# Output weights of the last batch loaded into free quarters of the input weights, with the order of all engines redone

## The chip, the core and the metric

The kernel runs on one core of a Trainium2 chip. The metric is the device time in microseconds (us). Five engines work side by side, each through its own list of instructions: TensorE (PE, with its weight loads listed apart as PEld), VectorE (DVE), ScalarE (ACT), GpSimd (POOL) and SyncE (SP). SP does nothing but issue the transfers between DRAM and the on-chip memory, one after the other; an instruction that waits holds up everything behind it on its engine.

## The reference, cut to what matters

Four batches of 8 heads, 768 positions, head width 64. Attention looks at a window of 16 positions and at one summary for each block of 32 (the largest key, the mean value). Its output x (768 x 512 in each batch) goes through a gated layer:

```python
h = np.maximum(x @ w_in, 0.0)                 # 512 -> 1024
u, v = h[..., :512], h[..., 512:]
v_n = (v - mu) / np.sqrt(var + 1e-06)         # over the 512
v_s = w_spatial @ v_n + b_spatial[:, None]    # mixes the 768 positions
return (u * v_s) @ w_out                      # 512 -> 512
```

## The kernel before, in words

Every operand of a large product is split into a high and a low part, and each product is made of three matmuls: high by high, high by low, low by high. `mm3` (L698 to L714) issues them, so all large products are at line 712: pv and pu are the halves v and u of x @ w_in, q the product with w_spatial, po the product with the output weights. Attention has lines of its own: s the scores (L401), p their softmax (L417 to L432), t a transposition of p (L443), x the product with the values (L462).

PE works on a batch's gated layer while the next batch's attention runs on the other engines. The gated layers of batches 1 to 3 make the product with w_spatial (`spatial_s`) from seven smaller products, whose combinations of w_spatial ("pieces" 0 to 6) were stored in DRAM as scr0 to scr6 and are loaded again in each batch, 1,152 KB each, into `arena`, a ring of three slots (`piece_load`). The load of a piece can be issued when the piece three before it has been used for the last time. The output weights wo were stored as scr7 and scr8 and are loaded again too. In the last batch before the change, the first half of them (d = 0 and 1) is an eighth piece of the ring; the other half (d = 2 and 3) goes into two tiles `wt` that take the place of a part of x.

The last batch also uses another form of the product x @ w_in, in which combinations of quarters of w_in are loaded from scw tensors into quarters of `win_h` and `win_l` (the high and low parts of w_in), and into `swv`. `gate` (L919 to L925) multiplies u into c and splits the result into gt for po.

What every engine does, and in which order, comes from one list of numbers, `ORDER`, over all operations (2,111 before), with `OTHER`, the set of operations that go to their second-choice engine. Buffers are given out in the same order. SP's transfers stand in this list as well; each waits, in turn, for its buffer and for the transfer issued eight before it.

Of the kernel before, what the change touches and what calls it, by code (L numbers as in the profile page):

```python
# [9 lines left out]
F32 = mybir.dt.float32  # L10
# [139 lines left out]
def tile_local_summary_attention_gmlp(ctx: ExitStack, tc: tile.TileContext, qT, kext, vpad, vnat, vT, w_in, w_sp, b_rep, w_out, out):  # L150
# [552 lines left out]
    def mm3(ps, n, steps, pri, *hold, first=True, skip=False):  # L703
# [185 lines left out]
    def spatial_s(b, pri, step):  # L889
# [65 lines left out]
        for n, i in enumerate((0, 1, 2, 3, 4, 5, 6, 7) if last else (0, 1, 2, 5, 6, 3, 4, 7, 8)):  # L955
# [38 lines left out]
        half = lambda x, d: (x, lambda w, cs: x.t[:, (d * 2 + w) * DM:(d * 2 + w + 1) * DM][:, cs])  # L994
        s["wo"] = [half(ar[7 + d // 2], d % 2) for d in range(2 if last else NC)]
        for d in range(2, NC if last else 2):
            x = Buf(att, [P, 2, 2 * CH], F32R, "x01l", f"wt{b}_{d}")
            mark("wt", b, d)
            dma(lambda x=x: x.t.rearrange("p w n -> p (w n)").bitcast(F32), scr[8][:, (d - 2) * 2 * DM:(d - 1) * 2 * DM], 512, pri + AR_AT,
                w=[x], r=[("scr", 8, w, 0) for w in range(2)] + [(u, f, c) for f in range(NC) for c in range(2)])  # L1000
            s["wo"].append((x, lambda w, cs, x=x: x.t[:, w, cs]))

    def proj_out(b, t, pri):
# [4 lines left out]
                             [gh[th, d][0], gl[th, d][0], gh[th, d][2], gl[th, d][2], s["wo"][d][0]]) for d in range(NC)] if b else [((lambda d=d: gh[th, d][1]()[:, o:o + P], lambda d=d: gl[th, d][1]()[:, o:o + P], lambda d=d: wo_h[:, d, cs], lambda d=d: wo_l[:, d, cs]),  # L1008
# [327 lines left out]
```

## Time and profile before

| | |
|---|---|
| median of 3 runs (lowest, highest) | 390.93 us (390.2, 393.24) |
| time of the profiled execution | 390.44 us |
| span in its trace | 388.6 us |
| PE busy | 377.7 us, 97% |
| PEld busy | 333.5 us, 86% |
| DVE busy | 280.6 us, 72% |
| ACT busy | 236.2 us, 61% |
| POOL busy | 154.2 us, 40% |
| granted TensorE clock | 1.00 in each stretch read below |

The span runs from the first to the last instruction; 1.8 us of the time lie around it. A busy share is an average over the whole span. In a timeline, each row gives the start, the length, the engine, the line and operation, the tiles, and in square brackets the idle time of the engine before it with what ended that. Matmuls overlap, so the length of one is more than what it adds: that is read from the distance between the starts.

### The profile page before, as it was taken

To read this page: it belongs to the slowest core of one execution; us is meant where nothing else is said; L and a number is where in the kernel's file an instruction comes from. 1 tells how busy PE (TensorE), PEld (TensorE's weight loads), DVE (VectorE), ACT (ScalarE), POOL (GpSimd) and SP (SyncE) were. 2 spreads that over 40 slices of the span, in tenths; PEclk is the share of its full clock that TensorE was granted. 3 is DMA by queue.
4 is the path that set the end of the run, shared out by engine and by line. 5 is a ranking of instruction groups with operands and counts; after the bars stand their busy time and mean duration, and the time that the engine had idled before them with its cause. 6 is when DMAs were issued, how large, how long until landed. Compare 5 with 4: busy or idle time off the path is not lost.

```text
span 388.6 us, 9377 instructions
## 1 busy us (share of the span) xinstructions
PE 377.7 (97%) x3382; PEld 333.5 (86%) x3382; DVE 280.6 (72%) x881; ACT 236.2 (61%) x716; POOL 154.2 (40%) x196
## 2 busy tenths in 40 slices
PE   8889999999999999999999999999999999999896
PEld 8658888888898888889998888899998799999885
DVE  4989898798876169787884658686787669785710
ACT  2999999876764756587463584756438555370212
POOL 4151455323573053424466143454644332623400
PEclk9999999999999999999999999999999999999999
DMA  8999997997788869979899737878899172949403
GB/s 286 406 281 279 287 347 212 293 258 237 266 230 251 279 216 340 314 231 331 312 306 335 179 102 253 296 216 326 284 291 316 76 253 91 339 167 357 188 30 133
DMA packets 38591, 99.05 MB, mean 255 GB/s; under 512 B 3601, under 2 KB 17937, under 8 KB 35217
## 3 DMA queue, kind: packets, MB, share of 16 engines
q1 hardware_dynamic: 38544, 98.45, 77.8%
q8 instruction: 27, 0.44, 0.5%
q14 instruction: 20, 0.16, 0.1%
HBM read 77.59 MB, written 20.84 MB: 253 GB/s over the span
## 4 chain that ended last, share of the span: by engine, by line
PE 79%; DMA 8%; DVE 5%; ACT 5%; issue 1%; SPq 1%; DVEq 0%; ACTq 0%
PE pv L712 16%; PE pu L712 16%; PE po L712 15%; PE q L712 13%; PE x L462 6%; PE s L401 5%; PE sp L712 4%; PE t L443 4%; DMA arena<-scr 4%; DMA vt<-in_vT_dram 3%; ACT p L421 3%; DMA k<-in_kext_dram 2%; DVE p L417 1%; DVE p L432 1%; SPq L216 1%
## 5 line engine op out<-in xcount | busy, mean ns | idle before, releaser
L421 ACT ACTIVATE p<-p,sums 128x120 f32<-128x120 f32 x192 | 73.9, 389 | 8.4 <-DVE sums L417 7.9
L432 POOL TENSOR_TENSOR p<-p,sums 128x480 f32<-128x480 f32 x34 | 34.8, 1040 | 52.0 <-DVE sums L428 44.8
L417 DVE CUSTOM_DVE_ANT_0 p<-s,mask 128x120 f32<-128x120 f32 x192 | 42.6, 276 | 10.0 <-PE s L401 10.0
L712 PE MATMUL po<-arena,gt 128*128 128x512 f32 (+1 forms) x168 | 40.3, 385 | 1.5 <-DMA arena<-scr 1.5
L712 PE MATMUL q<-arena,vnh 128*128 128x384 f32 x144 | 37.1, 338 | 0.0
L712 PEld LDWEIGHTS po<-arena,gt 128*128 128x128 f32 x168 | 30.3, 188 | 7.7 <-issue 1.8
L421 ACT ACTIVATION_READ_ACCUMULATOR p<-p,sums 128x1 f32 x192 | 36.8, 192 | 0.0
L712 PE MATMUL pu<-xh,win_h 128*128 128x512 f32 (+1 forms) x96 | 33.1, 345 | 0.0
L712 PE MATMUL pu<-xl,win_h 128*128 128x512 f32 (+1 forms) x96 | 32.4, 337 | 0.0
L712 PE MATMUL pu<-xh,win_l 128*128 128x512 f32 (+1 forms) x96 | 32.3, 337 | 0.0
L712 PE MATMUL q<-arena,wo_hl 128*128 128x384 f32 x144 | 29.9, 339 | 0.2 <-DMA arena<-scr 0.2
L712 PE MATMUL pv<-win_h,xh 128*128 128x512 f32 x72 | 29.9, 415 | 0.0
L712 PE MATMUL pv<-win_h,xl 128*128 128x512 f32 x72 | 28.2, 392 | 0.0
L712 PE MATMUL pv<-win_l,xh 128*128 128x512 f32 x72 | 28.2, 392 | 0.0
L443 PE MATMUL t<-ident,p 128*120 128x128 f32 x192 | 27.3, 274 | 0.9 <-POOL p L432 0.4
L462 PEld LDWEIGHTS x<-pt,ve 120*64 120x64 f32 x768 | 23.6, 138 | 5.2 <-issue 1.2
L222 ACT COPY pt<-t 120x512 f32<-120x512 f32 x36 | 20.8, 586 | 12.1 <-PE t L443 11.7
L921 POOL TENSOR_TENSOR c<-c,u 128x384 f32<-128x384 f32 x17 | 17.7, 1046 | 26.2 <-DVE c L938 17.0
L443 PEld LDWEIGHTS t<-ident,p 128*120 128x120 f32 x192 | 22.0, 137 | 5.6 <-POOL p L432 1.4
L462 PE MATMUL x<-pt,ve 120*64 120x64 f32 x768 | 25.5, 224 | 1.1 <-ACT ob_t3h L526 0.7
L712 PEld LDWEIGHTS q<-arena,vnh 128*128 128x128 f32 x144 | 25.6, 188 | 0.3 <-DVE sums L417 0.2
L712 PEld LDWEIGHTS q<-arena,wo_hl 128*128 128x128 f32 x144 | 24.9, 188 | 1.1 <-DVE ob_y L949 0.5
(274 smaller groups left out, 987.8 us busy)
## 6 DMA issues: line engine op xcount, KB each, us to landing
arena<-scr SPq DMA_DIRECT2D x21, 1152.0 KB, 6.3
k<-in_kext_dram SPq DMA_DIRECT2D x16, 544.0 KB, 7.7
qd<-in_qT_dram SPq DMA_DIRECT2D x24, 256.0 KB, 6.4
ve<-in_vpad_dram SPq DMA_DIRECT2D x24, 256.0 KB, 7.1
out_dram<-ob SPq DMA_DIRECT2D x23, 256.0 KB, 2.1
arena<-scr SPq DMA_DIRECT2D x5, 1024.0 KB, 7.6
vt<-in_vT_dram SPq DMA_DIRECT2D x12, 384.0 KB, 4.8
scr<-ct SPq DMA_DIRECT2D x12, 384.0 KB, 3.7
```

Source lines behind the costliest of these rows:

```text
L216: add(("SP", issue), lambda e: nc.sync.dma_start(out=out_() if callable(out_) else out_, in_=in_() if callable(in_) else in_), pri, w, r, ...
L222: (nc.scalar.copy if e == "ACT" else nc.vector.tensor_copy)(out=out_, in_=in_)
L401: nc.tensor.matmul(out=ps[a].t[r * QB:(r + 1) * QB, i * KW:(i + 1) * KW], lhsT=qt[hs, r, i], rhs=kts[r].t[hs, g * SEG:g * SEG + KW], start ...
L417: add(("DVE", 205), lambda e, i=i, mi=mi, a=a, pt=pt, k=k: nc.vector.tensor_tensor_reduce(out=at(pt, i), in0=ps[a].t[:, i * KW:(i + 1) * K ...
L421: add(("ACT", 380), lambda e, i=i, pt=pt, k=k: nc.scalar.activation(out=at(pt, i), in_=at(pt, i), func=AF.Exp, scale=-1.0, bias=st.t[:, 0, ...
L432: add(dict(DVE=590, POOL=950), lambda e, a=a, pt=pt: eng(e).tensor_tensor(out=four(pt), in0=four(pt), in1=st.t[:, 0, a * BPU:(a + 1) * BPU ...
L443: nc.tensor.transpose(out=ps.t[:KW, i * P:(i + 1) * P], in_=pt.t[:, i * KW:(i + 1) * KW], identity=ident)
L462: nc.tensor.matmul(out=x.t[a * D:(a + 1) * D, r * CH + n * QB:r * CH + (n + 1) * QB], lhsT=ve[buf][:, n, o:o + D], rhs=tt[a].t[:KW, n * P ...
L712: nc.tensor.matmul(out=ps.t[:, :n], lhsT=x, rhs=y, start=(first and j == i == 0), stop=(j == last and i == 2), skip_group_check=skip)
L921: add(two_ns(HT), lambda e: eng(e).tensor_mul(out=g.t[:, :HT], in0=g.t[:, :HT], in1=u.t[:, d, ts]), pri, w=[g], r=[u, (u, d, 0), (u, d, th ...
```

## The change

In the last batch, the output weights are no longer loaded into the ring and into `wt`. They come in eight transfers of 256 KB, high and low part of each d, into quarters of `win_h` and `win_l` whose last use is over; the ring has seven pieces. `mm3` gives its output a matching shape where the right operand has three dimensions (128 x 2 x 256), as these quarters have. In the last batch, `gate` waits for both halves of u. `ORDER` (now 2,116 operations) and `OTHER` are replaced as a whole, for all four batches.

```diff
@@ weight
-            return at, [*keys, *[f"wi{half}_{k}_0{w}" for k in range(int(n[2]) - 1, NC, 2) for w in "hl"]]
+            return at, [("home", half, n), *keys, *[f"wi{half}_{k}_0{w}" for k in range(int(n[2]) - 1, NC, 2) for w in "hl"]]
@@ mm3
+                o = ps.t[:, :n]
+                if len(rh.shape) == 3 > len(lh.shape):
+                    o = o.rearrange("p (k n) -> p k n", k=rh.shape[1])
-                    nc.tensor.matmul(out=ps.t[:, :n], lhsT=x, rhs=y, start=(first and j == i == 0), stop=(j == last and i == 2), skip_group_check=skip)
+                    nc.tensor.matmul(out=o, lhsT=x, rhs=y, start=(first and j == i == 0), stop=(j == last and i == 2), skip_group_check=skip)
@@ gate
-            add(..., r=[u, (u, d, 0), (u, d, th)], port=True)
+            add(..., r=[u, (u, d, 0), (u, d, 1 if last else th)], port=True)
@@ spatial_s
-        for n, i in enumerate((0, 1, 2, 3, 4, 5, 6, 7) if last else (0, 1, 2, 5, 6, 3, 4, 7, 8)):
+        for n, i in enumerate((0, 1, 2, 3, 4, 5, 6) if last else (0, 1, 2, 5, 6, 3, 4, 7, 8)):
...
-        s["wo"] = [half(ar[7 + d // 2], d % 2) for d in range(2 if last else NC)]
-        for d in range(2, NC if last else 2):
-            x = Buf(att, [P, 2, 2 * CH], F32R, "x01l", f"wt{b}_{d}")
-            dma(lambda x=x: x.t.rearrange("p w n -> p (w n)").bitcast(F32), scr[8][:, (d - 2) * 2 * DM:(d - 1) * 2 * DM], 512, pri + AR_AT,
-                w=[x], r=[("scr", 8, w, 0) for w in range(2)] + [(u, f, c) for f in range(NC) for c in range(2)])
+        if not last:
+            s["wo"] = [half(ar[7 + d // 2], d % 2) for d in range(NC)]
+            return
+        for d, (h, i, r, gone) in enumerate(((1, 1, 0, ("sw", 1, 4)), (0, 0, 0, ("home", 0, "a11")), (0, 0, 1, ("home", 0, "a12")), (0, 1, 0, ("sw", 0, 2)))):
+            base = h * DF + i * HD
+            for w, x in enumerate((win_h, win_l)):
+                at = (d % 2 * 2 + w) * DM
+                dma(x[:, r::2, base:base + HD].bitcast(F32), scr[7 + d // 2][:, at:at + DM].rearrange("p (k n) -> p k n", k=2), 256, pri + AR_AT,
+                    w=[("wt", d, w), gone], r=[("scr", 7 + d // 2, w, 0), *[("scw", h, n) for n in range(1, 5)]])
+            def of(w, cs, r=r, base=base):
+                x = (win_h, win_l)[w][:, r::2, base:base + HD]
+                return x if cs.stop - cs.start == DM else x[:, cs.start // HD]
@@ tables
 ORDER = [
-    0, 1, 2, 3, 6, 8, 7, 84, 9, 47, 10, 85, 48, 49, 108, 143, 101, 52, 11, 19, 25, 23, 13, 21, 17, 15, 54, 53, 12, 26, 24, 86, 18, 14, 87, 88, 89, 55,
+    1, 2, 6, 8, 7, 84, 9, 47, 3, 0, 10, 85, 48, 49, 108, 143, 101, 52, 53, 23, 24, 86, 21, 25, 13, 19, 14, 11, 17, 12, 22, 18, 26, 87, 15, 16, 54, 88,
...
```

Three places show what the new order does. The first is SP's queue in the last batch, from its last input-weight quarter to its last weight load (arena<-scr1 to scr6 are pieces, scr7 and scr8 the output weights). Before:

```order
L216 DMA win_l_124<-scw04_141 128x2x256
L216 DMA arena_125<-scr1_130 128x2304
L216 DMA arena_125<-scr2_131 128x2304
L216 DMA arena_125<-scr3_132 128x2304
L216 DMA wt3_3_4697<-scr8_137 128x1024
L216 DMA wt3_2_4717<-scr8_137 128x1024
L216 DMA arena_125<-scr4_133 128x2304
L216 DMA arena_125<-scr5_134 128x2304
L216 DMA arena_125<-scr6_135 128x2304
L216 DMA arena_125<-scr7_136 128x2048
```

After the change, the twelve rows that end with the last load of weights:

```order
L216 DMA arena_125<-scr2_131 128x2304
L216 DMA win_h_123<-scr8_137 128x2x256
L216 DMA win_l_124<-scw04_141 128x2x256
L216 DMA win_h_123<-scr7_136 128x2x256
L216 DMA win_l_124<-scr7_136 128x2x256 x2
L216 DMA arena_125<-scr3_132 128x2304
L216 DMA win_l_124<-scr8_137 128x2x256
L216 DMA win_h_123<-scr8_137 128x2x256
L216 DMA arena_125<-scr4_133 128x2304
L216 DMA arena_125<-scr5_134 128x2304
L216 DMA arena_125<-scr6_135 128x2304
L216 DMA win_l_124<-scr8_137 128x2x256
```

The two loads into `wt` and the eighth piece, which stood last, are gone. Eight loads of quarters stand between the pieces; the first of them, win_h_123<-scr7_136, is two rows ahead of this piece of the list. Nothing but the last low quarter stands behind piece 6 (scr6).

The second is PE at the end of batch 3's attention, up to its last product x3_2 (po2 are output tiles of batch 2; p3_2 and t3_2 the last softmax and its transposition, which pt3_2 carries to x3_2). Before:

```order
L712 MATMUL po2_5_4057<-arena_125,gt2_1_1_3822 128x512 x3
L712 MATMUL po2_5_4057<-arena_125,gt2_1_2_3959 128x512 x3
L443 MATMUL t3_2_1_1_4067<-ident_78,p3_2_1_1_3965 120x128 x4
L712 MATMUL po2_4_4040<-arena_125,gt2_1_2_3959 128x512 x3
L712 MATMUL po2_3_4047<-arena_125,ob_gt2_1_3_3982 128x512 x3
L443 MATMUL t3_2_0_0_4094<-ident_78,p3_2_0_0_3976 120x128 x4
L443 MATMUL t3_2_1_0_4099<-ident_78,p3_2_1_0_3967 120x128 x4
L443 MATMUL t3_2_0_1_4108<-ident_78,p3_2_0_1_3969 120x128 x4
L712 MATMUL po2_4_4040<-arena_125,ob_gt2_1_3_3982 128x512 x3
L712 MATMUL po2_5_4057<-arena_125,ob_gt2_1_3_3982 128x512 x3
L712 MATMUL po2_2_4139<-arena_125,gt2_0_0_4084 128x512 x3
L462 MATMUL x3_2_0_4152<-pt3_2_0_0_4150,ve0_148 64x64
```

After:

```order
L715 MATMUL po2_4_4037<-arena_125,gt2_1_2_3981 128x512 x3
L715 MATMUL po2_3_4054<-arena_125,gt2_1_1_3834 128x512 x3
L715 MATMUL po2_3_4054<-arena_125,gt2_1_2_3981 128x512 x3
L715 MATMUL po2_3_4054<-arena_125,ob_gt2_1_3_3958 128x512 x3
L443 MATMUL t3_2_1_0_4070<-ident_78,p3_2_1_0_3968 120x128 x4
L443 MATMUL t3_2_0_0_4092<-ident_78,p3_2_0_0_3966 120x128 x4
L715 MATMUL po2_5_4041<-arena_125,ob_gt2_1_3_3958 128x512 x3
L443 MATMUL t3_2_0_1_4105<-ident_78,p3_2_0_1_3971 120x128 x4
L443 MATMUL t3_2_1_1_4110<-ident_78,p3_2_1_1_3973 120x128 x4
L715 MATMUL po2_4_4037<-arena_125,ob_gt2_1_3_3958 128x512 x3
L715 MATMUL po2_0_4139<-arena_125,gt2_0_0_4080 128x512 x3
L462 MATMUL x3_2_0_4143<-pt3_2_0_0_4100,ve0_148 64x64
```

The first group of t stood behind 24 matmuls of po2, and now all four stand behind 30 of them, within one group of po2 of one another. Behind the last t there are 6 matmuls of po2, where there were 9. On DVE, three operations of gt2 and one of ob_t1 stood between p3_2_0_1 and the copy pt3_2_0_0; now that copy follows p3_2_0_1 directly, and the copy pt3_2_0_1, before on ACT, comes on DVE behind one operation of gt2.

The third is SP near the start (vt holds the values from which the block means come, ve the values for the product x, qd the queries, wi and vn parts of w_in and of the values). Before:

```order
L216 DMA wi0_2_280<-in_w_in_dram 128x1024
L216 DMA vn_277<-in_vnat_dram 128x1536
L216 DMA ve0_148<-in_vpad_dram 32x4x256
L216 DMA vt1_0_428<-in_vT_dram 128x768
L216 DMA ve0_148<-in_vpad_dram 64x4x256
L216 DMA qd0_146<-in_qT_dram 128x512
L216 DMA ve1_149<-in_vpad_dram 64x4x256
L216 DMA ve1_149<-in_vpad_dram 32x4x256
L216 DMA qd1_147<-in_qT_dram 128x512
```

After:

```order
L216 DMA wi0_2_283<-in_w_in_dram 128x1024
L216 DMA vn_280<-in_vnat_dram 128x1536
L216 DMA qd1_147<-in_qT_dram 128x512
L216 DMA vt1_0_439<-in_vT_dram 128x768
L216 DMA ve0_148<-in_vpad_dram 64x4x256
L216 DMA ve0_148<-in_vpad_dram 32x4x256
L216 DMA qd0_146<-in_qT_dram 128x512
L216 DMA ve1_149<-in_vpad_dram 64x4x256
L216 DMA ve1_149<-in_vpad_dram 32x4x256
```

The third load of qd1 stood last of the nine, and now stands ahead of vt1_0, all four of ve and qd0. It waits for the scores s0_1_1, which read the buffer that it fills.

In the last batch on PE, twelve matmuls of pu3_7_0 and pu3_5_0 (6 each, 128x384), which stood ahead of the q3_2, now stand among the q3_3, between the last use of the slot that piece 4 takes and the first use of piece 4.

## Rows read from the trace of the kernel before

**Rows 1.** Windows by stage: length, then busy us (x instructions) of each engine, PEclk, DMA share, GB/s.

```profile
0.00:40.00 40.00, 35.54 (x474) 28.55 (x474) 32.42 (x144) 31.55 (x107) 14.02 (x35) 1.00 0.98 316
40.00:290.00 250.00, 249.86 (x2325) 219.77 (x2323) 188.28 (x576) 161.63 (x488) 110.52 (x123) 1.00 0.84 269
290.00:310.00 20.00, 19.00 (x149) 15.90 (x148) 14.68 (x62) 13.29 (x54) 6.81 (x7) 1.00 0.66 202
...
350.00:370.00 20.00, 18.30 (x102) 17.41 (x102) 13.19 (x25) 4.01 (x8) 8.26 (x8) 1.00 0.69 260
```

**Rows 2.** Waits of PE, whole span: us in total, times, longest.

```profile
PE po L712 <- DMA arena<-scr: 1.5, 1, 1.5
PE s L401 <- DVE sums L428: 0.9, 1, 0.9
...
PE q L712 <- DMA arena<-scr: 0.2, 1, 0.2
```

**Rows 3.** Timeline of PE, end of the last batch.

```profile
356.58 0.34 PE L712 MATMUL q<-arena,vnl 128*128 128x384 f32 x1
357.13 3.36 PE L712 MATMUL q<-arena,wo_hl 128*128 128x384 f32 x18 [0.22 <-DMA arena<-scr]
...
366.09 0.51 PE L712 MATMUL q<-arena,vnh 128*128 128x384 f32 x2
366.44 0.34 PE L712 MATMUL q<-arena,vnl 128*128 128x384 f32 x1
368.26 3.68 PE L712 MATMUL po<-arena,gt 128*128 128x512 f32 x15 [1.48 <-DMA arena<-scr]
371.78 0.84 PE L712 MATMUL po<-wt,gt 128*128 128x512 f32 x3
372.46 0.84 PE L712 MATMUL po<-arena,gt 128*128 128x512 f32 x3
...
384.15 0.52 PE L712 MATMUL po<-wt,gt 128*128 128x256 f32 x3
384.51 0.52 PE L712 MATMUL po<-wt,ob_gt 128*128 128x256 f32 x3
```

**Rows 4.** Chain that ended last, its transfers at the end.

```profile
350.70 6.29 DMA arena<-scr
...
360.52 7.60 DMA arena<-scr
```

**Rows 5.** DMA issues by kind: count, KB each, median us to landing.

```profile
win_h<-scw SPq DMA_DIRECT2D x5, 256.0 KB, 3.4
win_l<-scw SPq DMA_DIRECT2D x5, 256.0 KB, 5.6
```

**Rows 6.** Timeline of PE at the end of batch 3's attention.

```profile
303.41 0.84 PE L712 MATMUL po<-arena,gt 128*128 128x512 f32 x3
304.95 2.09 PE L462 MATMUL x<-pt,ve 120*64 120x64 f32 x64 [0.70 <-ACT ob_t3h L526]
```

**Rows 7.** Timeline of DVE at the same place.

```profile
301.35 2.57 DVE L931 TENSOR_TENSOR gt<-c,gt 128x384 fp32r<-128x384 f32 x3
303.84 0.41 DVE L528 TENSOR_TENSOR ob_t<-xt,ob_t 128x256 fp32r<-128x256 f32 x1
304.17 0.68 DVE L222 COPY pt<-t 120x512 f32<-120x512 f32 x1
```

**Rows 8.** Timeline of SP near the start.

```profile
15.83 1.19 SPq L216 DMA_DIRECT2D vt<-in_vT_dram  x1
...
21.63 0.33 SPq L216 DMA_DIRECT2D qd<-in_qT_dram  x1
```

**Rows 9.** Timeline of PE near the start.

```profile
20.36 1.17 PE L401 MATMUL s<-k,qd 64*64 64x120 f32 x32 [0.93 <-DVE sums L428]
...
28.08 1.15 PE L462 MATMUL x<-pt,ve 120*64 120x64 f32 x32 [0.35 <-DVE sums L417]
```

**Rows 10.** Timeline of DVE near the start.

```profile
26.71 0.95 DVE L367 TENSOR_REDUCE vs_in<-vt 128x24 f32<-128x768 f32 x1 [0.58 <-DMA vt<-in_vT_dram]
```

More of the change, by code (lines that the diff above doesn't have):

```diff
@@ L920, in gate @@
             ts = slice(th * HT, (th + 1) * HT)
-            add(two_ns(HT), lambda e: eng(e).tensor_mul(out=g.t[:, :HT], in0=g.t[:, :HT], in1=u.t[:, d, ts]), pri, w=[g], r=[u, (u, d, 0), (u, d, th)], port=True)
+            add(two_ns(HT), lambda e: eng(e).tensor_mul(out=g.t[:, :HT], in0=g.t[:, :HT], in1=u.t[:, d, ts]), pri, w=[g], r=[u, (u, d, 0), (u, d, 1 if last else th)], port=True)
             if b == B - 1 and (th, d) in ((1, 0), (1, 1)):
@@ L993, in spatial_s @@
                 leave(m, 0, 1, 0)
-        half = lambda x, d: (x, lambda w, cs: x.t[:, (d * 2 + w) * DM:(d * 2 + w + 1) * DM][:, cs])
-        s["wo"] = [half(ar[7 + d // 2], d % 2) for d in range(2 if last else NC)]
-        for d in range(2, NC if last else 2):
-            x = Buf(att, [P, 2, 2 * CH], F32R, "x01l", f"wt{b}_{d}")
-            mark("wt", b, d)
-            dma(lambda x=x: x.t.rearrange("p w n -> p (w n)").bitcast(F32), scr[8][:, (d - 2) * 2 * DM:(d - 1) * 2 * DM], 512, pri + AR_AT,
-                w=[x], r=[("scr", 8, w, 0) for w in range(2)] + [(u, f, c) for f in range(NC) for c in range(2)])
-            s["wo"].append((x, lambda w, cs, x=x: x.t[:, w, cs]))
+        half = lambda x, d: ([x], lambda w, cs: x.t[:, (d * 2 + w) * DM:(d * 2 + w + 1) * DM][:, cs])
+        if not last:
+            s["wo"] = [half(ar[7 + d // 2], d % 2) for d in range(NC)]
+            return
+        s["wo"] = []
+        for d, (h, i, r, gone) in enumerate(((1, 1, 0, ("sw", 1, 4)), (0, 0, 0, ("home", 0, "a11")), (0, 0, 1, ("home", 0, "a12")), (0, 1, 0, ("sw", 0, 2)))):
+            base = h * DF + i * HD
+            for w, x in enumerate((win_h, win_l)):
+                mark("wt", d, w)
+                at = (d % 2 * 2 + w) * DM
[4 more added lines that the diff above has]
+                return x if cs.stop - cs.start == DM else x[:, cs.start // HD]
+            s["wo"].append(([("wt", d, 0), ("wt", d, 1)], of))
     def proj_out(b, t, pri):
@@ L1007, in proj_out @@
         steps = lambda cs: [((lambda d=d: gh[th, d][1]()[:, o:o + P], lambda d=d: gl[th, d][1]()[:, o:o + P], lambda d=d: s["wo"][d][1](0, cs), lambda d=d: s["wo"][d][1](1, cs)),
-                             [gh[th, d][0], gl[th, d][0], gh[th, d][2], gl[th, d][2], s["wo"][d][0]]) for d in range(NC)] if b else [((lambda d=d: gh[th, d][1]()[:, o:o + P], lambda d=d: gl[th, d][1]()[:, o:o + P], lambda d=d: wo_h[:, d, cs], lambda d=d: wo_l[:, d, cs]),
+                             [gh[th, d][0], gl[th, d][0], gh[th, d][2], gl[th, d][2], *s["wo"][d][0]]) for d in range(NC)] if b else [((lambda d=d: gh[th, d][1]()[:, o:o + P], lambda d=d: gl[th, d][1]()[:, o:o + P], lambda d=d: wo_h[:, d, cs], lambda d=d: wo_l[:, d, cs]),
                              [gh[th, d][0], gl[th, d][0], gh[th, d][2], gl[th, d][2], f"wo{d}h", f"wo{d}l"]) for d in range(NC)]
```

171 rows, old and new, of tables (ORDER, OTHER) are left out of this document.

## The prediction, as it was put down before the result

> **What bounds the kernel now.** The windows by stage come first [rows 1]. PE is busy for 249.86 of the 250 us from 40 to 290, at a granted clock of 1.00, so between these marks nothing but fewer or shorter matmuls could make the time shorter, and the change takes out none. What PE loses lies in three places: 4.46 us of the first 40 (where the DMA share is 0.98: the inputs are arriving), 1.00 us from 290 to 310, and 1.70 us from 350 to 370. The list of PE's waits [rows 2] then names the causes: the longest single one is po waiting 1.5 us for a transfer into the ring; others are between 0.2 and 0.9 us. So the room is small: 4.46 + 0.14 + 1.00 + 1.70 = 7.3 us at the very most, 1.9% of the time, and the first of these includes the start, where PE has no data yet. Last come the timelines of the places where a wait lies, since a share of busy time says nothing of them.
>
> **The end of the last batch: -2.0 us.** The step from one matmul to the next is read from starts: two 128x384 matmuls take 366.44 - 366.09 = 0.35 us, so 0.175 each; three 128x512 take 372.46 - 371.78 = 0.68, so 0.227 each; three 128x256 take 384.51 - 384.15 = 0.36, so 0.12 each [rows 3]. The last q starts at 366.44 and the first po at 368.26: 1.82, of which 0.175 is its own step, so 1.65 us are lost. The chain says why: the eighth piece, which holds half of the output weights, is issued at 360.52, when its slot comes free, and takes 7.60 us [rows 4]. That piece is gone. Its part comes in quarters, which are issued ahead of pieces 3 to 6, or just behind. The only one behind piece 6, a low quarter, can be issued when the q3_3 that frees piece 6's slot are done. From there to the first po there are 18 q with piece 4 and most of 36 more, some 50 x 0.175 = 8.8 us, and a quarter of this shape landed in 3.4 (high) or 5.6 us (low) [rows 5]. Some 3 us are left over, so the wait is not replaced.
>
> The other loss is 357.13 - 356.58 = 0.55, less a step of 0.175, so 0.38 us, for piece 4: its load takes 6.29 us [rows 4], and the 36 q between the release of its slot and its first use cover 36 x 0.175 = 6.3. Twelve pu of 128x384 now stand among these: 12 x 0.175 = 2.1 us of cover. That ends this wait and leaves about 2 us for the eight quarters, which share the engines. In all 1.65 + 0.38 = 2.0 us go. The bounds are 0 (another transfer is late instead) and 2.1.
>
> The bytes are the same 2 MB (1,024 KB and two of 512 KB before, eight of 256 KB now). What the pieces lose to them is bounded by the 2 us of cover. The DMA share is 0.69 from 350 to 370 and the last piece's 1,024 KB are no longer in it [rows 1, 4], so I count nothing. The Trainium skill, DMA: Bandwidth & Descriptors, section Measured, speaks against this part: it advises batches of at least 1 MiB for 75% of the peak, with 64 KB at 32%. Between those two, an estimate of 55% for 256 KB would make the 2 MB take some 2.6 us longer (8.7 against 6.1), and if all of that fell on a piece, 0.6 us would be lost beyond the cover; the sum would be 0.6 higher. No row shows 256 KB loads in such a group.
>
> **Two runs of 256 in place of 512 columns: 0.** Sixty po matmuls of the last batch (five tiles x four d x three) now read a right operand of 2 x 256 columns. No row shows one. The ends: as 512 in one run, 0.227; as two matmuls of 256, 0.24. That is 0 to 60 x 0.013 = 0.8 us. I take 0, since the number of columns is that of the first. The twenty-four po of 256 columns read one run, as before.
>
> **The gate that waits for both halves of u, and the buffers of x that `wt` no longer takes: 0.** All pu of the last batch stand ahead of the q that need the ring's last pieces, and the gates follow those; the 36 q behind piece 4 hide it. Without that cover, a gate would be late by a group of three pu, 3 x 0.175 = 0.5 us.
>
> **The end of batch 3's attention: -0.9 us.** The po before x3_2 start at 303.41 and end their three steps at 304.09; x3_2 starts at 304.95, so 0.86 us are lost [rows 6]. The profile names ACT, but ACT's operation had long been done: DVE's copy of pt runs from 304.17 to 304.85, right until x can start, and ahead of it stand three operations of gt and a cast, from 301.35 to 304.17 [rows 7]. In the new order that copy follows p3_2_0_1 directly, and only one gt (0.86 us, a third of 2.57) is between it and the other copy, so both are some 1.3 us earlier or more. Six po behind the last t (1.4 us) in place of nine cover a copy (0.68) and a gt. I take 0.9, between 0 (the other copy or the softmax itself is late) and 1.0, all that PE idles from 290 to 310.
>
> **The start: +0.5 us.** Here something gets worse. The load of qd1 that has to wait for s0_1_1 now stands ahead of vt, ve0, qd0 and ve1 on SP. Before, vt was issued at 15.83 and this qd1 at 21.63 [rows 8], right after the 32 s from 20.36 were over [rows 9]. So vt and what follows can be issued no earlier than about 22, some 6 us later. Against that, vt landed only at about 26.7, when DVE's wait for it ended [rows 10], 10.9 us after its issue: most of that it spent behind other bytes. A load without such a queue took 3.4 to 5.6 us [rows 5], so ve0, some 1.5 us behind vt, would land at 27 to 29.5, where x0 started at 28.08. And the 256 KB of qd1 now move ahead of it: at the 316 GB/s of that window, 0.8 us. On the other side, the wait of 0.58 us for vt on DVE [rows 10] no longer stands ahead of the softmax. Ends: -0.6 and +2.5; I take +0.5, near the moved bytes, since the engines are full there.
>
> **Everything between 40 and 290: +0.5 us.** The order is new there too, and PE idles 0.14 us. It can only lose. Ends are 0 and 3 (several waits); I take one wait of the middle size of the list, 0.5 [rows 2].
>
> **Sum.** 390.44 - 2.0 - 0.9 + 0.5 + 0.5 = **388.5 us**, 0.6% below the median of 390.93. The profiled execution lies 0.49 below that median, within the spread of the three runs, and I keep the sum as it is.
>
> **Rivals.**
> *All waits go, none comes* (0.2): the start gains 0.6 in place of losing 0.5 and the middle stays full. 390.44 - 2.0 - 0.9 - 0.6 = 386.9. For it: the order before leaves 0.14 us there, so an order without waits exists. Against: qd1's place on SP.
> *SP's wait drains the transfers at the start* (0.13): if what was issued up to 15 us has landed before 22, the engines idle, and ve0 lands at the late end. Start +2.5, sum 390.5. Decided by whether the DMA share falls in the windows from 20 to 30 us. The Trainium skill, DMA: Bandwidth & Descriptors, section Queues, rings and completion order, says that a semaphore is waited for on the issuing sequencer before dispatch, which is this rival's mechanism; the gap from one SP issue to the next in rows 8 agrees, but no row shows the engines idle for it.
> *The middle loses more* (0.14): waits of 2.5 us in place of 0.5, sum 390.5. The change then gives nothing. Also here: the po wait just moves to a quarter or a gate, so that the change doesn't do what it says.
> *Slower: a quarter holds back a piece* (0.13). On SP the quarters stand ahead of pieces 3 and 4, and each waits for the last pv or pu that reads what it overwrites (the third for pv3_2_5, the last of its kind). If that comes more than 2.1 us (the cover) after the piece's slot is free, the piece is late by the rest, and so are all behind it in the ring. A whole low quarter's 5.6 us in its way would cost 5.6 - 2.1 = 3.5 us: 392.0; a second one for piece 4 up to 394.5. Against it: the pu and pv that free the quarters stand ahead of the q that free the slots.
>
> **Chances and range.** My forecast, 387.3 to 389.7, has 0.4. Less than 1% (3.9 us) either way can't be told from no change with certainty. Faster by over 1% means below 387.0: most of the first rival, 0.2. Slower means over 394.8: the far end of the last, and a double mishap, 0.07. The rest is 0.73. The range from 386.0 to 392.5 takes in the bounds of the single terms and the near part of the last rival, and leaves some 0.1 on either side.
>
> **What would show it.** The end: no PE wait for a transfer behind 350, po starting 0.2 us after the last q, and a po step of 0.227 on the quarters (0.24 says that the two runs cost). Batch 3: x3_2 starting within 0.3 us of the last po step. The start: x0 between 28.2 and 29.5, DMA share near 1.0 from 20 to 30; below 0.9 shows the drained transfers. The middle: PE idle under 1 us from 40 to 290. I am wrong if the middle or the start loses over 2 us, or if pieces 3 to 6 are waited for.

## The result, and the profile after

| | before | changed kernel |
|---|---|---|
| median of 20 runs (lowest, highest) | 392.6 us (389.61, 396.06) | 394.06 us (391.99, 397.77) |
| time of the profiled execution | 390.44 us | 393.27 us |
| span in its trace | 388.6 us | 391.5 us |

The changed kernel is slower: its time is 1.0056 times that of the kernel before, with a 95% interval from 1.0037 to 1.0075 (written [1.0037, 1.0075] from here on). This ratio and those below come from the fast runs alone, without those over 1.5% above the fastest of their kernel, so they are not the quotients of the medians. The forecast was 0.6% faster, and 394.06 lies above its range. The windows by stage of the changed kernel answer [rows 1], with the same columns; one more stretch stands at the end.

```profile
0.00:40.00 40.00, 33.77 (x446) 27.79 (x446) 30.93 (x143) 30.26 (x103) 15.01 (x35) 1.00 0.91 301
40.00:290.00 250.00, 246.45 (x2218) 216.19 (x2217) 188.88 (x576) 160.56 (x488) 104.55 (x113) 1.00 0.81 263
290.00:310.00 20.00, 19.80 (x217) 17.01 (x215) 16.13 (x61) 12.66 (x48) 9.53 (x9) 1.00 0.82 261
...
350.00:370.00 20.00, 20.00 (x117) 20.00 (x117) 12.36 (x22) 5.94 (x10) 10.81 (x11) 1.00 0.73 267
```

PE's busy time is the first number behind each length. The end gained what was promised: 20.00 - 18.30 = 1.70 us from 350 to 370, and 0.80 from 290 to 310. The rest lost more: 35.54 - 33.77 = 1.77 in the first 40 us, and 249.86 - 246.45 = 3.41 from 40 to 290. The balance is -2.68 us, and the span grew by 2.9.

PE's waits after the change, whole span, as in [rows 2]:

```profile
PE q L715 <- DVE wq L572: 1.8, 1, 1.8
...
PE s L401 <- DMA qd<-in_qT_dram: 1.6, 2, 1.4
PE x L462 <- DMA ve<-in_vpad_dram: 1.5, 1, 1.5
PE x L462 <- DMA arena<-scr: 1.1, 1, 1.1
...
PE q L715 <- DMA arena<-scr: 0.2, 1, 0.2
```

The 1.5 us wait of po at the end is gone, and four waits of 1.1 to 1.8 us have come that were absent or, for s on qd, 0.4 us long. That wait of s lies near the start: SP now issues the first load of qd0 behind that of k0_2, and it lands at 8.8 us, not at 6.7. Two of the names on the right are not the true ones. In the program, the q of the first row waits for the load of piece 3 in batch 2, and the x of the fourth for the second half of `ve0` for x2_2. The timeline of PE has their places, and those of x0 and the next x at the start:

```profile
29.42 1.15 PE L462 MATMUL x<-pt,ve 120*64 120x64 f32 x32 [1.49 <-DMA ve<-in_vpad_dram]
...
32.36 0.82 PE L462 MATMUL x<-pt,ve 120*64 120x64 f32 x21 [0.47 <-ACT p L421]
...
212.46 0.74 PE L462 MATMUL x<-pt,ve 120*64 120x64 f32 x18 [1.10 <-DMA arena<-scr]
...
286.55 0.59 PE L715 MATMUL q<-arena,vnh 128*128 128x384 f32 x2 [1.75 <-DVE wq L572]
...
301.14 0.47 PE L715 MATMUL po<-arena,gt 128*128 128x512 f32 x1 [0.20 <-DMA arena<-scr]
...
309.11 0.84 PE L715 MATMUL po<-arena,gt 128*128 128x512 f32 x3
309.88 0.51 PE L462 MATMUL x<-pt,ve 120*64 120x64 f32 x10
...
370.45 0.33 PE L715 MATMUL q<-arena,vnl 128*128 128x384 f32 x1
370.62 0.39 PE L715 MATMUL po<-win_h,gt 128*128 128x512 f32 x1
...
376.43 0.62 PE L715 MATMUL po<-win_h,gt 128*128 128x512 f32 x2
376.88 0.39 PE L715 MATMUL po<-win_l,gt 128*128 128x512 f32 x1
377.11 0.62 PE L715 MATMUL po<-win_h,gt 128*128 128x512 f32 x2
```

The last rows answer [rows 3] and [rows 6]: x3_2 starts 0.77 us behind the three po ahead of it, whose own steps take 0.68; the first po starts 0.17 us behind the last q; and three po on the quarters take 377.11 - 376.43 = 0.68 us, 0.227 each, as on one run of 512 columns. The high quarters landed in 3.8 us (columns as in [rows 5]):

```profile
win_h<-scr SPq DMA_DIRECT2D x4, 256.0 KB, 3.8
```

SP's timeline at the start, which answers [rows 8], and around batch 2's pieces:

```profile
21.55 0.33 SPq L216 DMA_DIRECT2D qd<-in_qT_dram  x1
21.92 0.43 SPq L216 DMA_DIRECT2D vt<-in_vT_dram  x1
22.40 1.35 SPq L216 DMA_DIRECT2D ve<-in_vpad_dram  x2
...
276.72 0.32 SPq L216 DMA_DIRECT2D arena<-scr  x1
277.36 0.32 SPq L216 DMA_DIRECT2D scw<-wq  x1
...
291.72 0.32 SPq L216 DMA_DIRECT2D arena<-scr  x1
292.09 0.43 SPq L216 DMA_DIRECT2D scw<-wq  x1
```

At the start, `vt` now goes out at 21.92 in place of 15.83. In batch 2, the load of piece 3 goes out at 276.72 and that of piece 8 (scr8) at 291.72, each with the store of a 512 KB scw tensor 0.4 to 0.6 us behind it. How long they took, from the list of issues of these moments:

```profile
arena<-scr SPq DMA_DIRECT2D x1, 1152.0 KB, 9.7
...
arena<-scr SPq DMA_DIRECT2D x1, 1024.0 KB, 9.3
```

The medians of the profile's page hide this, and a load that is in time costs nothing however slow it is. What counts is the distance from issue to the moment that PE is ready, against the time the load takes. For three loads that PE comes close to, worked out from such rows of both kernels (PE ready is the start of the first reader less its idle time):

| load | kernel | issued | PE ready | distance | load took | PE waited |
|---|---|---|---|---|---|---|
| second `ve0` load of x2_2 | before | 198.35 | 209.22 | 10.9 | 10.7 | 0 |
| | changed | 200.31 | 211.36 | 11.0 | 11.9 | 1.10 |
| piece 3, batch 2 | before | 272.03 | 280.86 | 8.8 | 5.5 | 0 |
| | changed | 276.72 | 284.80 | 8.1 | 9.7 | 1.75 |
| piece 7, batch 2 | before | 285.70 | 292.70 | 7.0 | 6.6 | 0 |
| piece 8, batch 2 | changed | 291.72 | 300.94 | 9.2 | 9.3 | 0.20 |

The kernel before has margins of 0.2 and 0.4 us at two of its three loads, and 3.3 us at piece 3. That PE was full there did not mean that these two loads had room.

### The profile page after: what moved, and what is told of

It is laid out like the page before. It is cut to its first block, busy times and chain, and to the rows that moved or that the text cites. A ratio compares the mean times of both kernels' runs of the same rounds, so it can differ in the third digit from the quotient of the medians.

```text
span 391.5 us, 9390 instructions
## 1 busy us (share of the span) xinstructions
PE 377.9 (97%) x3390; PEld 334.8 (86%) x3390; DVE 282.4 (72%) x881; ACT 235.6 (60%) x711; POOL 162.6 (42%) x201
## 4 chain that ended last, share of the span: by engine, by line
PE 82%; DMA 10%; DVE 3%; ACT 1%; POOL 1%; issue 1%; SPq 1%; POOLq 0%; DVEq 0%
PE po L715 16%; PE pu L715 16%; PE pv L715 16%; PE q L715 12%; DMA arena<-scr 7%; PE sp L715 6%; PE x L462 5%; PE t L443 5%; PE s L401 4%; DMA qd<-in_qT_dram 2%; DMA ve<-in_vpad_dram 2%; ACT p L421 1%; POOL p L432 1%; DVE p L417 1%; SPq L216 1%
## 5 line engine op out<-in xcount | busy, mean ns | idle before, releaser
L432 POOL TENSOR_TENSOR p<-p,sums 128x480 f32<-128x480 f32 x34 | 35.9, 1074 | 65.2 <-DVE sums L428 53.3
L417 DVE CUSTOM_DVE_ANT_0 p<-s,mask 128x120 f32<-128x120 f32 x192 | 42.7, 277 | 11.1 <-PE s L401 10.9
L715 PE MATMUL po<-arena,gt 128*128 128x512 f32 x126 | 30.9, 393 | 0.2 <-DMA arena<-scr 0.2
L715 PE MATMUL q<-arena,wo_hl 128*128 128x384 f32 x144 | 30.8, 341 | 0.0
L222 ACT COPY pt<-t 120x512 f32<-120x512 f32 x35 | 19.8, 586 | 15.7 <-PE t L443 14.6
L715 PE MATMUL pv<-win_h,xl 128*128 128x512 f32 x72 | 28.2, 392 | 0.0
L715 PE MATMUL pv<-win_l,xh 128*128 128x512 f32 x72 | 28.2, 392 | 0.0
L715 PEld LDWEIGHTS po<-arena,gt 128*128 128x128 f32 x126 | 23.2, 188 | 5.4 <-issue 0.6
L924 POOL TENSOR_TENSOR c<-c,u 128x384 f32<-128x384 f32 x18 | 18.5, 1038 | 19.8 <-DVE c L941 14.4
L401 PE MATMUL s<-k,qd 64*64 64x120 f32 x768 | 23.9, 267 | 2.4 <-DMA qd<-in_qT_dram 1.6
```

Source lines behind the costliest of these rows:

```text
L222: (nc.scalar.copy if e == "ACT" else nc.vector.tensor_copy)(out=out_, in_=in_)
L401: nc.tensor.matmul(out=ps[a].t[r * QB:(r + 1) * QB, i * KW:(i + 1) * KW], lhsT=qt[hs, r, i], rhs=kts[r].t[hs, g * SEG:g * SEG + KW], start ...
L417: add(("DVE", 205), lambda e, i=i, mi=mi, a=a, pt=pt, k=k: nc.vector.tensor_tensor_reduce(out=at(pt, i), in0=ps[a].t[:, i * KW:(i + 1) * K ...
L432: add(dict(DVE=590, POOL=950), lambda e, a=a, pt=pt: eng(e).tensor_tensor(out=four(pt), in0=four(pt), in1=st.t[:, 0, a * BPU:(a + 1) * BPU ...
L715: nc.tensor.matmul(out=o, lhsT=x, rhs=y, start=(first and j == i == 0), stop=(j == last and i == 2), skip_group_check=skip)
```

## Experiments: which part of the order loses

In the diffs, `before` is the kernel before's list of operations, carried over into the numbers of the changed kernel, and `after` is the changed kernel's. Each ratio is to the kernel before, run on the same chip at the same time.

**1. The quarters alone.** The order before everywhere, with the eight quarter loads put into it.

```diff
-ORDER = after
+ORDER = before, with the eight loads of quarters ahead of pieces 3 and 4 and behind piece 6
```

> The order of before on all engines, with the output weights of the last batch loaded in quarters as in the changed kernel (five of the eight loads ahead of pieces 3 and 4, two ahead of piece 4, one behind piece 6). Theory A (the change's loss lies in the order of SP's transfers in the first 290 us, its gain in the loads at the end): PE no longer waits 1.65 us ahead of the first po, the 0.4 us ahead of piece 4 stay, start and middle are as before: ratio to before 0.996 (-1.6 us). Theory B (quarters of 256 KB with rows of 1 KB cost more than they save, by delaying pieces 3 to 6): PE waits for a piece by 1.5 us or more, ratio 1.000 or above.

Measured: 390.77 us against 391.57, ratio 0.9983 [0.9959, 1.0007]; span 387.7. From 350 to 370 PE was busy for 19.72 us, against 18.30 [rows 1], and the po wait was gone. The loads do their work with no new order at all. Of the 1.42 us gained there the span kept 0.9, partly since the start of this profile had a wait of 0.7 us for `ve` that the one before has not. In the time, the move on its own can't be told from no change.

**2. The new order from 285 us on, and from there alone.**

```diff
-ORDER = after
+ORDER = before[:1600] + [n for n in after if n not in before[:1600]]
```

> The order of before up to about 285 us (its first 1,600 operations), then the order of the changed kernel with its loads. Theory A: start and middle keep before's PE idle (0.14 us from 40 to 285), the end has the changed kernel's: no wait ahead of x3_2 (0.9 us less) and none for piece 4 and the first po (1.7 to 2.0 us less): ratio to before 0.993 (-2.5 to -2.9 us), faster than both. Theory E (the gain at the end belongs to what stands ahead of it in the new order, and is lost when batch 2's end comes in the old order): ratio 0.998 or above.

Measured: 388.91 us against 391.57, ratio 0.9932 [0.9908, 0.9956]; span 386.6. So the quarters with the new order from 285 us on are worth 0.7%, what the prediction had for its two places (2.9 of 390.44 us, 0.74%); in the profile, these two give 1.39 us (350 to 370) and 0.45 (290 to 310), and the span is 2.0 us shorter. Of what the changed kernel lost, little stands behind 285 us: here it is a wait of 0.55 us for piece 8.

**3 and 4. The new order from 42 us on, and from 219 us on.**

```diff
+ORDER = before[:260] + [n for n in after if n not in before[:260]]
...
+ORDER = before[:1240] + [n for n in after if n not in before[:1240]]
```

> The order of before up to about 42 us (its first 260 operations), then the changed kernel. Theory A2 (what the change loses in the first 40 us, 1.8 us of PE time, belongs to the order of that stretch as a whole): PE busy in 0 to 40 us near 35.5 as before, where the changed kernel has 33.8; waits after 200 us stay; ratio to before 1.001. Theory G (those 1.8 us only show up earlier or later, and the middle absorbs them): ratio 1.005.

> The order of before up to about 219 us (its first 1,240 operations), then the changed kernel. Theory A2: start as before, no wait ahead of x2_2 near 212 us; of the changed kernel's waits only those ahead of batch 2's piece 3 (1.8 us) and of a pu (0.5 us) are left: ratio 0.998 to 0.999 (-0.5 us). With the kernel that changes over at 285 us (0.9932) the difference is 2.0 us, the price of the stretch from 219 to 285. Theory H (the waits between 219 and 285 come from delays before them): ratio 0.994, no wait ahead of piece 3.

Measured: 1.0032 [0.9996, 1.0069] from 42 us on, span 390.5; 1.0002 [0.9963, 1.0040] from 219 us on, span 387.4. With the changed kernel itself and experiment 2 this makes a ladder: 1.0056 (new from 0), 1.0032 (from 42), 1.0002 (from 219), 0.9932 (from 285). The four fall in order, but only the last step, 0.7% for the stretch from 219 to 285 us, is clear of the intervals; the other two are not told from nothing. The trace from 219 us on does not show that loss: the load of piece 3 took 6.4 us with the store 0.64 us behind it as in the changed kernel, PE did not wait for it, and from 40 to 290 us PE idled for 1.24 us, not 3.55. That execution (389.3 us) was the fastest of its ten, whose median is 391.3. So these waits come and go from one execution to the next, and one profile does not give what a stretch costs.

## Experiments: what is late there

**5. One transfer of the start put back.** SP's load of qd1, which waits for s0_1_1 and which the prediction blamed, goes behind `vt` and `ve`.

```diff
-L216 DMA qd_147<-in_qT_dram 128x512
 L216 DMA vt_0<-in_vT_dram 128x768
...
 L216 DMA ve_149<-in_vpad_dram 32x4x256
+L216 DMA qd_147<-in_qT_dram 128x512
```

> The changed kernel with one transfer moved on SP: the load of qd1 that waits for s0_1_1 goes back behind vt, ve0, qd0 and ve1. Theory A: the transfers no longer run dry between 20 and 30 us (DMA share from 0.87 to 1.0), x0 starts near 28.1 again where it started at 29.4, and 1.3 to 1.8 us of the 1.8 lost in the first 40 us come back: ratio to before 1.0010 to 1.0025 where the changed kernel has 1.0056. Theory C (the loss at the start comes from the other engines' new order, DVE's and ACT's softmax): x0 stays at 29.4, ratio 1.005.

Measured: 1.0060 [1.0035, 1.0084], span 391.5. The wait at x0 went and PE lost the same further on: busy for 32.83 us of the first 40, against 33.77. The load of qd1 was not the cause by itself; that theory fell. Nor is it shown that the start loses because the transfers run dry: from 20 to 30 us the DMA share was 1.06 here (second row, columns as in [rows 1]) and 0.87 in the changed kernel (first row), and over the first 40 us PE lost more here:

```profile
20.00:30.00 10.00, 8.48 (x100) 5.48 (x99) 9.63 (x37) 9.65 (x33) 5.36 (x5) 1.00 0.87 272
...
20.00:30.00 10.00, 8.77 (x117) 5.88 (x121) 8.79 (x35) 9.93 (x36) 5.37 (x5) 1.00 1.06 292
```

**6. The whole start of SP put back.** SP's first 26 transfers in the order before (four of them change places), the other engines as in the changed kernel.

```diff
-L216 DMA k_2<-in_kext_dram 128x1088
 L216 DMA qd_146<-in_qT_dram 128x512
+L216 DMA k_2<-in_kext_dram 128x1088
...
-L216 DMA qd_147<-in_qT_dram 128x512
 L216 DMA vt_0<-in_vT_dram 128x768
...
+L216 DMA qd_147<-in_qT_dram 128x512
```

> The changed kernel, with the first 26 transfers of SP in the order of before (q0 ahead of the third load of k0, the 32-row part of ve0 ahead of vt, qd1 behind ve1); all other engines as in the changed kernel. Theory A3 (the loss of the first 40 us is SP's order as a whole, of which the one load of qd1 was only a part): PE busy in 0 to 40 us 35.3 or more, ratio 1.001. Theory C2 (the loss comes from the order on DVE and ACT, whose softmax and copies stand differently): PE busy stays at 33 to 34, ratio 1.005.

Measured: 1.0037 [1.0001, 1.0072], span 390.2. In the profile, PE's first 40 us are whole again, 35.66 busy (35.54 before), and the DMA share from 20 to 30 us, which had fallen from 1.07 to 0.87 in the changed kernel, is back at 1.07. So 1.9 us came back there, and yet the span fell by 1.3. Two more traces have this list at the start (experiments 10 and 11): 33.06 and 34.67 us. The three with the changed kernel's own list have 32.51 to 33.77, and the seven with the whole start of before 34.73 to 35.69. By the means (34.5 against 33.1 us) the list is worth some 1.4 us, and a single execution is no measure of it. The timeline of PE shows where the rest went:

```profile
299.82 0.47 PE L715 MATMUL po<-arena,gt 128*128 128x512 f32 x1 [1.19 <-DMA arena<-scr]
```

PE came earlier to piece 8, whose load took 10.3 us, and waited for it. A gain ahead of a late load is given back at the load.

**7. The other half of `ve0` for x2_2 issued earlier**, ahead of two loads of qd.

```diff
+L216 DMA ve_148<-in_vpad_dram 32x4x256
 L216 DMA qd_147<-in_qT_dram 128x512
 L216 DMA qd_146<-in_qT_dram 128x512
-L216 DMA ve_148<-in_vpad_dram 32x4x256
```

> The changed kernel with one transfer moved on SP: the second load of ve0 for x2_2 goes ahead of the two loads of qd that stand before it. Theory A: the wait of 1.1 us ahead of x2_2 near 212 us, which the profile puts down to a load into the ring, is for this load of 128 KB, and vanishes (0 to 0.2 left): ratio 1.003 where the changed kernel has 1.0056. Theory D (it is the load into the ring that is late, as the profile names it): the wait stays at 1.1, ratio 1.0056.

Measured: 1.0051 [1.0029, 1.0073]. The wait at x2_2 fell from 1.10 to 0.42 us, and a wait of 0.56 appeared ahead of it, so that little came back and the name of this load rests on the program more than on the run; the load of piece 3 took 10.0 us and PE waited 2.1 for it. The profiled execution was the slowest of its ten (397.28 us, median 393.62), so its later waits are no measure. Half a microsecond at one place was too little to be told from nothing in the time.

**8. The store beside piece 3 moved** behind the loads of pieces 7 and 4.

```diff
 L216 DMA arena<-scr_132 128x2304
-L216 DMA scw_140<-wq_3 128x1024
 L216 DMA arena<-scr_136 128x2048
 L216 DMA arena<-scr_133 128x2304
+L216 DMA scw_140<-wq_3 128x1024
```

> The changed kernel with one transfer moved on SP: the store of scw03 (512 KB, to DRAM), which is issued 0.6 us behind batch 2's piece 3, goes behind pieces 7 and 4. Theory F (the store takes the transfer engines' time from the piece, which takes 9.3 to 9.7 us in place of 6.1): the piece lands in 6 to 7 us, the wait of 1.4 to 2.1 us ahead of it vanishes, ratio 1.001 to 1.002. Theory I (the piece is slow for other reasons; its transfers scatter by 2 us and more whatever stands beside them): the wait stays at 1 us or more, ratio 1.005.

Measured: 1.0000 [0.9966, 1.0034], against 1.0056 with the store in its place. Piece 3 took 7.2 us, not 9.7, and the wait of 1.75 us was gone. Piece 4, which now had the store 0.37 us behind it, took 6.1 us. (The profiled execution, 394.82 us against a median of 391.85, had longer waits elsewhere, 2.1 us at the start and 1.9 at 208.)

**9. A store put beside a load, in the kernel before.** The reverse of 8, and the cleanest of all: only the store of scw02 moves, from 2.5 us behind the load of piece 7 to right behind it.

```diff
 L216 DMA arena<-scr_136 128x2048
+L216 DMA scw_139<-wq_2 128x1024
 L216 DMA ve_148<-in_vpad_dram 64x4x256
 L216 DMA ve_149<-in_vpad_dram 32x4x256
-L216 DMA scw_139<-wq_2 128x1024
```

> The kernel before with one transfer moved: the store of scw02, issued 2.5 us behind the load of batch 2's piece 7 (285.70 us, 6.6 us long, TensorE ready for it 7.2 us after the issue), is issued right behind that load. Theory 'a store issued right behind a load lengthens it': the load takes 9 to 10.5 us, as the last such load did in the changed kernel (9.3) and in three of its variants (9.6 to 10.6), TensorE waits 1.8 to 3.3 us for it, and the ratio is 1.005 to 1.008. Rival 'the load is as long as the traffic of that stretch makes it': it takes 6 to 7.5 us, TensorE waits below 0.4 us, and the ratio is 0.998 to 1.002.

Measured: 1.0016 [0.9981, 1.0050], span 390.4. The load and the wait came as expected of the theory; the time did not. The load, from the list of issues:

```profile
arena<-scr SPq DMA_DIRECT2D x1, 1024.0 KB, 9.1
```

PE, from the timeline of where it waits for this load:

```profile
295.58 3.65 PE L712 MATMUL po<-arena,gt 128*128 128x512 f32 x8 [2.04 <-ACT p L421]
```

The windows of 3 us that begin there (columns as in [rows 1]):

```profile
293.00:296.00 3.00, 0.96 (x5) 0.63 (x4) 2.72 (x15) 3.00 (x17) 1.60 (x2) 0.95 1.11 259
296.00:299.00 3.00, 3.00 (x8) 2.34 (x7) 1.80 (x5) 2.95 (x16) 0.40 (x1) 0.50 1.12 241
```

The load took 9.1 us in place of 6.6, and po waited 2.04 us for it (the name on the right is again another's). Behind the wait PE ran at half clock: PEclk 0.50, that is 1.2 of 2.4 GHz, and eight po took 3.65 us, where eight steps of 0.227 [rows 3] are 1.8. Instruction by instruction, this kernel was 0.65 us behind the kernel before ahead of that wait, 2.9 behind it, 4.6 when the clock was back, and 3.5 by 365 us. Then the end gave back 1.7: the last piece there took 5.0 us and not the 7.60 of [rows 4], and po's wait of 1.48 [rows 3] was gone. So in this pair of traces, where the store alone has moved, a load of 1,024 KB took 2.5 us longer with a store of 512 KB right behind it, and the time shows only what no later slack takes back. It is one execution of each, and both hold a case against the theory: piece 4, with the store of scw04 0.42 us behind it, took 6.1 us in the kernel before and 6.0 here.

**10. Four repairs of SP's list at once.** The changed kernel with 6, 7 and 8, and the store of scw02 moved away from piece 8's load.

```diff
 L216 DMA arena<-scr_137 128x2048
-L216 DMA scw_139<-wq_2 128x1024
 L216 DMA ve_149<-in_vpad_dram 64x4x256
...
 L216 DMA ve_148<-in_vpad_dram 64x4x256
+L216 DMA scw_139<-wq_2 128x1024
```

> The changed kernel with four of SP's transfers put elsewhere and the order of all other work kept: its first 26 transfers in the order of the kernel before, the second ve0 load of x2_2 ahead of two qd loads, the store of scw03 behind the loads of pieces 7 and 4 of batch 2, and the store of scw02 behind the four ve loads that follow piece 8. Theory 'transfers that come just too late': each loss that the profiles of single repairs showed comes back, 1.9 us at the start, 0.4 to 0.9 at x2_2, 1.8 at piece 3, and piece 8 lands before TensorE is there, so that the wait of 1.2 us that took back the gain of the start alone stays away; the span is 386.7 to 388.0 us and the ratio 0.992 to 0.997, that of the order from 290 us on. Rival 'the new order is longer in itself' (TensorE's own work or the engines that feed it): the waits move to other instructions, the span stays over 389.5 and the ratio over 0.999.

Measured: 0.9981 [0.9957, 1.0006], between the two expectations. Its profiled execution, 393.5 us, was the slowest of its twelve (median 390.56): PE was busy for 33.06 us of the first 40, where experiment 6, with the same list of SP there, had 35.66. It shows, though, that I had moved one burden, not removed it: the store of scw03 now went out right behind piece 4, whose load took 9.2 us with a distance of 8.7, and PE waited for that. And the load of piece 8 took 10.8 us, longer than that of piece 3, 4, 7 or 8 of batch 2 in any other trace, though the next store now went out 4.7 us behind it; PE, held up for 1.1 us just ahead, did not wait for it. A store right behind is not all that makes a load long. SP's issues, PE, and the load of piece 8:

```profile
284.34 0.32 SPq L216 DMA_DIRECT2D arena<-scr  x1
284.71 0.42 SPq L216 DMA_DIRECT2D scw<-wq  x1
```

```profile
293.66 3.37 PE L715 MATMUL q<-arena,wo_hl 128*128 128x384 f32 x18 [0.61 <-DMA arena<-scr]
```

```profile
arena<-scr SPq DMA_DIRECT2D x1, 1024.0 KB, 10.8
```

**11. The same with that store beside a load that has room**, piece 7, which PE needs 15 us after its issue.

```diff
 L216 DMA arena<-scr_136 128x2048
+L216 DMA scw_140<-wq_3 128x1024
 L216 DMA arena<-scr_133 128x2304
-L216 DMA scw_140<-wq_3 128x1024
```

> As the kernel with four of SP's transfers put elsewhere, but the store of scw03 goes one place earlier, between the loads of pieces 7 and 4: beside piece 7, which TensorE needs only 15.9 us after its issue, and away from piece 4, which it needs after 8.7. Theory 'transfers that come just too late': piece 4 takes 7 to 8.5 us there in place of 9.2, the wait of 0.6 us for it goes, and with it the wait of 1.1 us of the next po if the late buffer of scw03's source was behind that; pieces 3 and 8 stay without a wait; the span is 387 to 388.5 us where the start does not lose again, and the ratio 0.992 to 0.997. Rival 'the new order is longer in itself': waits of the same sum stand somewhere else between 280 and 310 us and the ratio stays at 0.998 or above.

Measured: 390.58 us against 392.22, ratio 0.9956 [0.9924, 0.9987]; span 387.6, 3.9 us below that of the changed kernel. PE, DVE, ACT and POOL have the changed kernel's instructions in the changed kernel's order, but for one warm-up matmul at the start; in SP's list, seven transfers stand elsewhere. Its windows by stage:

```profile
0.00:40.00 40.00, 34.67 (x468) 28.39 (x470) 31.98 (x145) 31.21 (x105) 15.01 (x35) 1.00 0.98 314
40.00:290.00 250.00, 248.59 (x2268) 218.44 (x2266) 191.15 (x580) 161.73 (x487) 104.37 (x113) 1.00 0.81 265
290.00:310.00 20.00, 20.00 (x221) 17.41 (x218) 14.95 (x62) 13.20 (x50) 11.10 (x12) 1.00 0.85 260
```

The loads of pieces 4 and 8, from the list of issues:

```profile
arena<-scr SPq DMA_DIRECT2D x1, 1152.0 KB, 6.6
...
arena<-scr SPq DMA_DIRECT2D x1, 1024.0 KB, 8.7
```

Between 283 and 304 us no wait of PE is listed. From 1.0056 to 0.9956 with no arithmetic touched: what the change lost against the kernel before, it lost on SP's list. The rival, that the new order of the other engines is longer in itself, wanted 0.998 or above. The repair is not complete: PE still idles for 1.41 us from 40 to 290, where the kernel before has 0.14.

**12. Experiment 2 with the store of scw02 behind the `ve` loads**, as in 10.

> The kernel that takes the new order from 285 us on alone, and in it the store of scw02, which stands 0.4 us behind the load of piece 8 of batch 2, behind the four ve loads that follow. Theory 'a store issued right behind a load lengthens it': the load of piece 8, 9.6 us there, takes 6.6 to 8 us, TensorE's wait of 0.55 us for it goes, the span falls by 0.4 to 0.6 us to about 386.1 and the ratio is 0.990 to 0.993. Rival 'the load is as long as the traffic of that stretch makes it': it takes 9 us or more, the wait stays, the ratio is that of the kernel without the move, 0.993.

Measured: 388.54 us against 392.08, ratio 0.9915 [0.9884, 0.9946]; span 386.8. In experiment 2, SP issues the load of piece 8 and the store, PE waits, and the load takes 9.6 us (timelines of SP and of PE, list of issues):

```profile
285.95 0.32 SPq L216 DMA_DIRECT2D arena<-scr  x1
286.32 0.42 SPq L216 DMA_DIRECT2D scw<-wq  x1
```

```profile
295.71 0.47 PE L715 MATMUL po<-arena,gt 128*128 128x512 f32 x1 [0.55 <-DMA arena<-scr]
```

```profile
arena<-scr SPq DMA_DIRECT2D x1, 1024.0 KB, 9.6
```

In this kernel, SP's issues and the load:

```profile
287.26 0.32 SPq L216 DMA_DIRECT2D arena<-scr  x1
289.28 2.37 SPq L216 DMA_DIRECT2D ve<-in_vpad_dram  x4
291.75 1.46 SPq L216 DMA_DIRECT2D scw<-wq  x1
```

```profile
arena<-scr SPq DMA_DIRECT2D x1, 1024.0 KB, 5.5
```

The same load takes 5.5 us in place of 9.6, and po's wait for it is gone. Between those two points of the program this kernel made up 0.7 us on the one of experiment 2, which is too little for the ratios to tell the two apart; ahead of them it was 1.3 us later, which is why the spans are level. Its ratio is the lowest of all the kernels here, clearly below those of the two that the case began with.

## Why the prediction was wrong, step by step

Of the 5.6 us between the forecast 388.5 and 394.06, 1.7 are the kernel before's own: its median was 390.93 in three runs and 392.6 in twenty. By the ratio the change costs 2.2 us, where 2.4 us of gain were forecast.

**The end of the last batch, -2.0: right.** 1.70 us from 350 to 370 and no wait behind 350 in the changed kernel; 1.39 us there in experiment 2. The quarters were not late; the rival that one of them holds back a piece did not happen. The prediction's estimate from the Trainium skill, DMA: Bandwidth & Descriptors, section Measured, that 256 KB transfers would cost 0.6 us more, was not borne out: no wait for a piece stands behind 350.

**Two runs of 256 columns, 0: right.** 0.227 us a step.

**The end of batch 3's attention, -0.9: right.** 0.80 us from 290 to 310, and x3_2 right behind the po.

**The start, +0.5: wrong in size.** It cost 1.77. The place and the load were named, the price was not believed: "what was issued up to 15 us has landed before 22, the engines idle" had 0.13, with a DMA share below 0.9 from 20 to 30 us as the sign. It was 0.87, but experiment 5, with 1.06, lost more, so that this is what costs is not shown. x0 started at 29.42, inside the 28.2 to 29.5 that I gave, but I priced only x0. The next x, at 32.36 where it was 30.23, and the transfers behind lost as well, and experiment 5 shows that they lose on their own when x0 does not: it took four of the first 26 transfers, not one load, to bring most of it back (experiments 6, 10 and 11).

**Everything between 40 and 290, +0.5: this step failed.** It cost 3.4 where the sum had 0.5. I had written "it can only lose" and then taken one wait of middle size, since PE idled for 0.14 us before and I read that as room. I did not set the loads' distances against their durations. The trace of before shows margins of 0.2 and 0.4 us at two loads; a new order that moves everything by a microsecond was likely to meet some of them. In the changed kernel's trace two waits, 1.10 at x2_2 and 1.75 at piece 3, are 2.85 of the 3.4 us; most of the rest is 0.45 of a pu that waits for DVE. Behind 290 comes a third load, piece 8: 0.20 us there, and up to 1.5 in another trace (experiment 3). Nor did I read, in SP's new list, that stores had come to stand right behind two of these loads. That was there to be read without any run, but not what it costs: experiments 8 and 9 give some 2.5 us for a load, and piece 4 of the kernel before shows that it can also be nothing.

**The rivals.** "SP's wait drains the transfers" and "the middle loses more" were priced at 390.5 each, as if only one could come. The second came, by the new order of SP, and of the first its sign and most of its price (1.77 of 2.5 us), though not shown to be by its mechanism. Put together in the prediction's own sum they make 390.44 - 2.0 - 0.9 + 2.5 + 2.5 = 392.5, where the profiled execution took 393.27. Treating them as exclusive kept the slower side small. The sentence on semaphores that the first of them takes from the Trainium skill stands in another section of that page than the one named, Anatomy of one DMA.

**What stays open.** How long a load takes. For the pieces 3, 4, 7 and 8 of batch 2 in all fourteen traces, 23 loads with a store up to 0.64 us behind them took 5.8 to 10.6 us, with a median of 8.6; 33 with the next store 1.7 us behind or later took 5.1 to 10.8, with a median of 7.2. So the store behind makes a long load likelier, and is neither needed nor enough. Piece 4, issued 0.42 us ahead of the store of scw04 by the same list, took 6.1 us before, 6.0 in experiment 9 and 8.5 in experiment 2. Bytes in flight from earlier transfers differ, but no run separates them. Open as well is which waits make the ladder's step from 1.0002 to 0.9932, since the one trace from 219 us on has few of them.

## What to carry to other kernels

When an order is redone as a whole, list for each load the distance from its issue to the moment that its reader is ready, and the time it took: a busy TensorE does not say that there is room, and a margin of 0.2 us can become a wait. Put stores beside loads that have 15 us, not beside those that have 8: with that and three more repairs, seven transfers moved on one queue, the ratio fell by 1% here, more than the 0.7% of the new end. Take more than one trace before a single load is blamed. Mend all late loads together, since a gain ahead of one that is late is given back at it.

## What was not expected of the hardware

A load can be longer with a store issued right behind it. The load of 1,024 KB took 6.6 us with the store of 512 KB 2.5 us behind, 9.1 with it 0.4 us behind (experiment 9), and 9.6 and 5.5 us in the other pair (12). That it is the store that does it is argued from these two pairs, one execution of each kernel, and other loads with a store as close took 6 us. The Trainium skill, DMA: Bandwidth & Descriptors, section Queues, rings and completion order, says that each engine consumes descriptors in ring order, and that a later one may still finish its write before an earlier one. The order of landing in experiment 9 agrees with the first, the load at 295.45 and the store at 296.73 us; what the store costs the load does not follow from either.

A wait of 2.04 us on PE cost another 1.7 us afterwards, while the granted clock stood at 0.50 in the 3 us behind it (experiment 9). In the trace of experiment 8 the clock also fell to 0.50 behind waits of 2.12 and 1.91 us. But a wait of 2.09 us in experiment 7 was followed by 1.00, so not every such wait costs this, and the changed kernel's wait of 1.75 us at 286.55 was followed by 1.00 too.
